# Swapping the operands of the products of keys' features with values: features stationary, values moving in 17 columns a head

## The chip, the cores and the metric

The kernel runs on one core of one Trainium2 chip. The metric is device time in microseconds (us) of one execution; the kernel before has a median of 490.55 us over three runs (489.4, 490.55 and 490.56).

## The reference, cut to what matters

The result mixes a linear attention `a` and a squared-ReLU feed-forward layer `b` with a gate of each row: `g * a + (1 - g) * b`. There are 2048 rows of 512 numbers, 32 heads of 16, and 1792 hidden units. The change touches the two sums over all rows, `kv` and `z`, in the attention:

```python
pk = jnp.einsum("bhsd,hdf->bhsf", k, w_phi)
phi_k = jnp.concatenate([_softmax(pk, axis=-1), _softmax(-pk, axis=-1)], axis=-1)   # 32 features a head
...
kv = jnp.einsum("bhsf,bhsd->bhfd", phi_k, v)     # per head 32 x 16
z  = jnp.einsum("bhsf->bhf", phi_k)              # per head 32
num = jnp.einsum("bhqf,bhfd->bhqd", phi_q, kv)
den = jnp.einsum("bhqf,bhf->bhq", phi_q, z)[..., None] + 1e-6
o = num / den
...
h = jnp.einsum("bsd,df->bsf", x, w1) + b1        # feed-forward, 512 to 1792
h = jnp.where(h > 0, h, 0) ** 2
b = jnp.einsum("bsf,fd->bsd", h, w2) + b2        # and back to 512
```

## The kernel before

All work is recorded first and ordered afterwards. A `Plan` object takes every operation of TensorE (PE), VectorE (DVE), ScalarE (ACT), GpSimd (POOL) and of the DMA queues of SyncE (SP) and ACT, finds what depends on what, and sets the order with a list scheduler that holds a table of lengths; PE's products go in groups, and at each step the scheduler takes the earliest startable of the next five groups. Some operations may go to either DVE or POOL (`nc.either`), and some DMAs to either queue (`nc.queues`); the scheduler picks. So a length that changes in one place can move operations elsewhere. All recorded operations carry line 359 in the profile, and one tells them apart by tiles.

The large products (the feed-forward and the projections) are made of three fp32r products of high and low parts (`h` and `l` in the tile names), and by a Strassen scheme (the `p1` to `p7` of the code). They write the banks uA, uE, uB (two of them), vA, vB, vE and kv, each 128 x 512.

The first half computes hidden units and, merged into it, keys and values for pairs of row blocks. For each of eight pairs of 128-row blocks the features of the keys stand in a tile `e` or `ez` (128 rows x 32 heads x 32 features) and the values in `vext` (128 rows x 32 heads x 17, the 17th column being one, so that the same product also gives `z`). `kv_burst` then makes 64 small fp32 products of them (two row blocks x 32 heads) into bank kv, four heads at a time in the four 32-column strips of the array, and adds the bank to the running sums in `kvs`. In the kernel before, the stationary operand is 32 columns of `vext`, starting at the head's first and reaching past its 17th, and the features are the 32 moving columns; in the bank a head has values along partitions and features along columns, so 17 of its 32 partitions mean something.

After the last burst, `kv_done` (line 724 and following) writes `z`, which stands on four partitions of `kvs`, to a row in DRAM (`zrow`) with two small DMAs, reads it back broadcast to 128 partitions into the two `vext` tiles (they are free by then) with two DMAs, turns `kvs` by two transposes on PE into a bank, and copies the sums from there into `kvb`, in four copies, block by block. The second half computes the queries' features chunk by chunk: `do_q` (product and exponentials), `transposed` (POOL multiplies by the broadcast z into `ez`, DVE sums and scales, a transpose to `tb`, then 12 DMAs and 4 ACT copies to `phiT`), `do_n` (products of `kvb` with `phiT`) and `attend`, all merged into the down projection of the feed-forward.

Of the kernel before, what the change touches and what calls it, by code (L numbers as in the profile page):

```python
# [10 lines left out]
AF = mybir.ActivationFunctionType  # L11
ALU = mybir.AluOpType
# [5 lines left out]
P = 128  # L18
S, D, H, DH, F = 2048, 512, 32, 16, 1792
# [5 lines left out]
NG = 8  # L25
VW = DH + 1
# [345 lines left out]
def tile_gated_mix(ctx: ExitStack, tc: tile.TileContext, xT, xn, wqT, wkT, wphi, wv, wo, w1, b1, w2, b2, gw, out):  # L372
    nc = Plan(tc.nc)
# [14 lines left out]
    def turn(*tags):  # L388
        i = turns[tags] = turns.get(tags, -1) + 1
        return banks[tags[i % len(tags)]]  # L390

    bank = lambda: turn("vA", "vB", "vE", "kv")
# [23 lines left out]
    const = lambda name, *shape: sbuf.tile([P, *shape], F32, tag=name, name=name)  # L416
    ident = const("ident", P)
# [4 lines left out]
    inv, eps, rest = (const(n, NB * NC) for n in ("inv", "eps", "rest"))  # L422
    kvb = const("kvb", NG, 2 * DH)
    tc.nc.gpsimd.memset(kvb, 0.0)
    kvs = const("kvs", 2 * P)
    tc.nc.gpsimd.memset(kvs, 0.0)
    zrow = dram.tile([2 * D], F32, name="zrow")
    xkept = dram.tile([6, 2, P, SB], F32, name="xkept")
# [270 lines left out]
    def kv_burst(v):  # L699
        n = 8 * v[0] + 2 * v[1]  # L700
        ps = banks["kv"]
        nc.product()
        for m in range(2):
            phi, ve = st["phi", n + m], vext[m]
            for i in range(NG):
                for j in range(4):
                    h = 8 * (i % 4) + 4 * (i // 4) + j
                    nc.tensor.matmul(ps[32 * j:32 * j + 32, 32 * i:32 * i + 32], ve[:, h * VW:h * VW + 32],
                                     phi[:, 32 * h:32 * h + 32], start=(m == 0 and i == 0), stop=(m == 1),
                                     skip_group_check=True)  # L710
        nc.vector.tensor_tensor(kvs, kvs, ps[:, :2 * P], ALU.add)

    def kv_done():
        zr = zrow.rearrange("(i q j f) -> q j i f", i=4, q=2, f=32)
        for q in range(2):
            nc.scalar.dma_start(zr[q], kvs[DH::32, q * P:(q + 1) * P].rearrange("p (i f) -> p i f", f=32))
        for half in range(2):
            nc.scalar.dma_start(vext[half][:, :D], zrow[half * D:(half + 1) * D].partition_broadcast(P))
        kvt = bank()
        nc.product()  # L720
        for i in range(2):
            nc.tensor.transpose(kvt[:, i * P:(i + 1) * P], kvs[:, i * P:(i + 1) * P], ident)
        kt = kvt[:, :2 * P].rearrange("p (g v) -> p g v", v=32)
        for j in range(4):
            s = slice(32 * j, 32 * j + 32)
            nc.vector.tensor_copy(kvb[s, :, DH * (j % 2):DH * (j % 2 + 1)], kt[s, :, :DH])

# [245 lines left out]
    def run(seq):  # L975
        for u, p in seq:
            if p == "burst":
                kv_burst(u)
            else:
                (v_step if len(u) == 3 else u_step)(u, p)  # L980
# [30 lines left out]
    fold("q", wqT, [t[:, k * D:(k + 1) * D] for k in range(NK)], load(ring(), wphi))  # L1011
    run(seq[-4:])
    kv_burst((1, NC - 1, "kv"))


# [6 lines left out]
    at = [0, 1, 5, 8, 11, 13, 16, 19, 22, 24, 27, 30, 33, 35, 38, 41]  # L1022
    wq_ready()
    when(1, kv_done)
    when(5, wo_ready)
    for i in range(NB):
        when(at[4 * i], gates, ORDER_B[i])
    for p in range(8):
# [3 lines left out]
        s = max(at[2 * p + 1], 2)  # L1032
# [3 lines left out]
    for t in range(NT):  # L1036
        for f in steps.get(t, ()):
            f()
        i, f = divmod(t, NF)
# [80 lines left out]
```

## Time and profile before

| | |
|---|---|
| runs | 489.4, 490.55, 490.56 us; median 490.55 |
| profiled execution | 490.21 us, of which the span of the profile is 488.4 us |
| PE busy | 482.6 us, 99% of the span, 3538 matmul records |
| DVE, ACT, POOL busy | 385.0, 251.2 and 160.1 us |
| granted TensorE clock | 1.000 of full speed over the span |
| DMA | 108.66 MB, mean 222 GB/s |

The time of the profiled execution is 1.8 us longer than its span, for what lies outside the first and last instruction. An fp32 product is two LDWEIGHTS and two MATMUL records; an fp32r product is one of each. Starts of instructions are in us from the span's start. A record's length is from its start to its modelled end, and successive matmuls overlap, so what a product costs is read from the distance between starts.

### The profile page before, as it was taken

Reading aid. Unit: us, or ns where it says so; the run is one execution under the profiler, and the core shown is the slowest. Engines: PE = TensorE matmul, PEld = TensorE weight load, DVE = VectorE, ACT = ScalarE, POOL = GpSimd, SP = SyncE. Lnnn points to the kernel's source line nnn. Section 1 sums busy time; section 2 is a strip of 40 time slices with the busy share of each in tenths; the row PEclk is TensorE's granted clock in tenths of the full one; section 3 lists DMA queues with packets and bytes.
Section 4 is the critical chain, followed back from the end, with each engine's and each line's share of the span. In section 5 each row is a group of like instructions: output and inputs, shape, how many; then the busy total and the mean of one; then the engine's idle time right before and its main releaser. Section 6 shows DMA issues by size and latency. Waiting matters only on the chain.

```text
span 488.4 us, 9588 instructions
## 1 busy us (share of the span) xinstructions
PE 482.6 (99%) x3538; PEld 389.2 (80%) x3538; DVE 385.0 (79%) x572; ACT 251.2 (51%) x447; POOL 160.1 (33%) x129
## 2 busy tenths in 40 slices
PE   9999999999999999999899999999999999999997
PEld 4878888888888888888788788787878788788786
DVE  3997999999987686969796799987795768996023
ACT  5897976579856664787510704133435213361210
POOL 1343165439520341246240434431621504261000
PEclk9999999999999999999999999999999999999999
DMA  7999999753787989898878576554317362354602
GB/s 275 382 401 364 374 329 344 268 175 131 243 267 274 313 258 326 275 321 305 279 214 226 138 266 185 194 172 119 119 41 192 136 180 91 89 159 137 229 25 86
DMA packets 65735, 108.66 MB, mean 222 GB/s; under 512 B 8216, under 2 KB 17688, under 8 KB 65688
## 3 DMA queue, kind: packets, MB, share of 16 engines
q1 hardware_dynamic: 60240, 102.66, 62.5%
q10 hardware_dynamic: 5416, 5.38, 4.2%
q8 instruction: 28, 0.46, 0.4%
q14 instruction: 19, 0.16, 0.1%
q0 software_dynamic: 32, 0.01, 0.0%
HBM read 60.30 MB, written 41.42 MB: 208 GB/s over the span
## 4 chain that ended last, share of the span: by engine, by line
PE 93%; DVE 3%; DMA 1%; ACT 1%; issue 1%; SPq 1%
PE uB L359 26%; PE uA L359 14%; PE uE L359 14%; PE vA L359 11%; PE vB L359 10%; PE kv L359 9%; PE vE L359 9%; DMA KT30h<-in_w 1%; SPq L359 1%; DVE oh L359 0%; DVE O1l L359 0%; DVE tb L359 0%; DVE KT31h L359 0%; DVE O0l L359 0%; DVE KB221l L359 0%
## 5 line engine op out<-in xcount | busy, mean ns | idle before, releaser
L359 POOL TENSOR_TENSOR ez<-e,vext 128x512 f32<-128x512 f32 x32 | 41.8, 1327 | 97.3 <-ACT e L359 85.2
L359 ACT ACTIVATE e<-e 128x512 f32<-128x512 f32 x54 | 32.0, 624 | 40.2 <-DVE e L359 40.1
L359 ACT ACTIVATE phiT<-tb 32x512 f32<-32x512 f32 x32 | 20.2, 630 | 52.2 <-DMA phiT<-tb 49.7
L359 DVE TENSOR_REDUCE sm<-e 128x64 f32<-128x1024 f32 x27 | 32.7, 1209 | 17.5 <-ACT e L359 17.3
L359 ACT ACTIVATE row<-row 128x512 f32<-128x512 f32 x56 | 34.0, 625 | 0.4
L359 POOL TENSOR_TENSOR row<-row,b2b 128x512 fp32r<-128x512 f32 (+1 forms) x12 | 17.0, 1419 | 38.3 <-ACT b2b L359 34.5
L359 DVE TENSOR_REDUCE ends<-vA 128x32 f32<-128x512 f32 x26 | 16.6, 681 | 9.7 <-PE vA L359 9.6
L359 POOL TENSOR_TENSOR row<-row,wo 128x512 fp32r<-128x512 f32 x10 | 14.0, 1401 | 27.7 <-ACT wo L359 27.7
L359 ACT ACTIVATE O0h<-ring 128x512 fp32r<-128x512 f32 x17 | 10.7, 627 | 21.9 <-DMA row<-in_wo 13.7
L359 DVE TENSOR_TENSOR e<-e,w 128x1024 f32<-128x1024 f32 x16 | 21.6, 1351 | 0.3
L359 DVE TENSOR_REDUCE dz<-ez 128x64 f32<-128x1024 f32 x16 | 19.3, 1206 | 3.0 <-POOL ez L359 3.0
L359 DVE STREAM_TRANSPOSE tb<-e 128x1024 f32<-128x1024 f32 x16 | 19.7, 1231 | 1.1 <-DMA O1l<-hkept 1.0
L359 DVE RECIPROCAL r<-sm 128x64 f32<-128x64 f32 x32 | 17.4, 544 | 0.4
L359 ACT ACTIVATE O1h<-ring 128x512 fp32r<-128x512 f32 x17 | 10.7, 628 | 12.7 <-PE uB L359 8.5
L359 ACT ACTIVATE wo<-row 128x512 fp32r<-128x512 f32 x17 | 10.6, 625 | 9.2 <-DMA hkept<-wo 9.1
L359 DVE TENSOR_TENSOR e<-e,r 128x1024 f32<-128x1024 f32 x11 | 14.0, 1273 | 0.1
L359 POOL TENSOR_TENSOR O1l<-ring,O1h 128x512 fp32r<-128x512 f32 x9 | 12.4, 1378 | 4.2 <-ACT O1h L359 4.2
L359 DVE TENSOR_TENSOR O0l<-ring,O0h 128x512 fp32r<-128x512 f32 x14 | 9.8, 704 | 4.5 <-ACT O0h L359 4.3
L359 ACT ACTIVATE oh<-vB 128x512 fp32r<-128x512 f32 x8 | 4.7, 593 | 15.7 <-PE vE L359 15.7
L359 DVE TENSOR_TENSOR row<-row,b2b 128x512 fp32r<-128x512 f32 (+1 forms) x12 | 8.1, 691 | 5.8 <-ACT b2b L359 5.8
L359 POOL TENSOR_TENSOR KB210h<-KB210h,KB211h 128x256 f32<-128x256 f32 x1 | 6.9, 6883 | 17.6 <-DVE KB211h L359 17.6
L359 DVE TENSOR_TENSOR O1l<-ring,O1h 128x512 fp32r<-128x512 f32 x8 | 6.3, 786 | 8.0 <-ACT O1h L359 8.0
(1157 smaller groups left out, 1701.3 us busy)
## 6 DMA issues: line engine op xcount, KB each, us to landing
hkept<-row SPq DMA_DIRECT2D x56, 256.0 KB, 4.9
ring<-hkept SPq DMA_DIRECT2D x24, 256.0 KB, 4.3
hkept<-b2b SPq DMA_DIRECT2D x16, 256.0 KB, 4.0
hkept<-wo SPq DMA_DIRECT2D x16, 256.0 KB, 3.6
xn<-in_xn SPq DMA_DIRECT2D x16, 256.0 KB, 3.8
O0h<-hkept SPq DMA_DIRECT2D x16, 256.0 KB, 3.2
O0l<-hkept SPq DMA_DIRECT2D x16, 256.0 KB, 3.5
O1h<-hkept SPq DMA_DIRECT2D x16, 256.0 KB, 4.4
```

What stands on the lines that cost most here:

```text
L359: call(*map(real, op.args), **{k: real(a) for k, a in op.kw.items()})
```

## The change

`kv_burst` swaps the operands: 32 features of a head are stationary and the head's 17 columns of `vext` move. The sums of a head now stand with features along partitions and 17 values along columns, eight heads beside each other on each strip of 32 partitions, and `kvs` has 136 columns and not 256. `kv_done` no longer turns `kvs`: `kvb` is filled by four copies straight from `kvs`. `z` now stands down the partitions, in column 16 of each group of 17, so it is turned by one transpose of 128 x 8 on PE, copied by ACT into a new tile `zt` (8 x 128), and written to `zrow` with one DMA. The two broadcast reads into `vext` stay.

```diff
-    kvs = const("kvs", 2 * P)
+    kvs = const("kvs", NG * VW)
+    zt = const("zt", P)
...
             phi, ve = st["phi", n + m], vext[m]
-            for i in range(NG):
-                for j in range(4):
-                    h = 8 * (i % 4) + 4 * (i // 4) + j
-                    nc.tensor.matmul(ps[32 * j:32 * j + 32, 32 * i:32 * i + 32], ve[:, h * VW:h * VW + 32],
-                                     phi[:, 32 * h:32 * h + 32], start=(m == 0 and i == 0), stop=(m == 1),
+            for b in range(NG):
+                for a in range(4):
+                    h = 8 * a + b
+                    nc.tensor.matmul(ps[32 * a:32 * a + 32, b * VW:(b + 1) * VW], phi[:, 32 * h:32 * h + 32],
+                                     ve[:, h * VW:(h + 1) * VW], start=(m == 0 and b == 0), stop=(m == 1),
                                      skip_group_check=True)
-        nc.vector.tensor_tensor(kvs, kvs, ps[:, :2 * P], ALU.add)
+        nc.vector.tensor_tensor(kvs, kvs, ps[:, :NG * VW], ALU.add)
 
     def kv_done():
-        zr = zrow.rearrange("(i q j f) -> q j i f", i=4, q=2, f=32)
-        for q in range(2):
-            nc.scalar.dma_start(zr[q], kvs[DH::32, q * P:(q + 1) * P].rearrange("p (i f) -> p i f", f=32))
+        kv = kvs.rearrange("p (b v) -> p b v", v=VW)
+        ps = bank()
+        nc.product()
+        nc.tensor.transpose(ps[:NG, :P], kv[:, :, DH], ident)
+        nc.scalar.activation(zt[:NG, :], ps[:NG, :P], AF.Copy)
+        nc.scalar.dma_start(zrow.rearrange("(a b f) -> b a f", a=4, f=32), zt[:NG, :].rearrange("b (a f) -> b a f", f=32))
         for half in range(2):
             nc.scalar.dma_start(vext[half][:, :D], zrow[half * D:(half + 1) * D].partition_broadcast(P))
-        kvt = bank()
-        nc.product()
-        for i in range(2):
-            nc.tensor.transpose(kvt[:, i * P:(i + 1) * P], kvs[:, i * P:(i + 1) * P], ident)
-        kt = kvt[:, :2 * P].rearrange("p (g v) -> p g v", v=32)
-        for j in range(4):
-            s = slice(32 * j, 32 * j + 32)
-            nc.vector.tensor_copy(kvb[s, :, DH * (j % 2):DH * (j % 2 + 1)], kt[s, :, :DH])
+        for a in range(4):
+            s = slice(32 * a, 32 * a + 32)
+            nc.vector.tensor_copy(kvb[s, :, DH * (a % 2):DH * (a % 2 + 1)], kv[s, :, :DH])
```

The scheduler's length of a small product is the same for 17 and 32 moving columns, but the shorter addition to `kvs` and the new steps of `kv_done` move other work. On PE three places differ: the shapes, the third burst (12 products later than before), and the stretch after the last burst. There, on PE, the two transposes (`vB<-ident,kvs`) stood behind the query product of the first chunk (into vA). Before:

```order
L359 MATMUL vA<-XS31l_3138,XA121h_1461 128x512 [waits DVE_49]
L359 MATMUL vA<-XS31h_3129,XA121l_1594 128x512
L359 MATMUL vB<-ident,kvs 128x128 x2
L359 MATMUL vE<-XS20h_3102,XA110h_1416 128x512
L359 MATMUL vE<-XS20l_3117,XA110h_1416 128x512
```

Now the one transpose stands ahead of both query products, directly behind the twelve products of the down projection that follow the burst, and six more of these, with the next hidden tile (O1h, O1l), come ahead of the queries:

```order
L359 MATMUL uB_73<-KB110h_2674,O0l_2663 128x512
L359 MATMUL vB<-ident,kvs 8x128 [waits DVE_49]
L359 MATMUL uA<-KB111h_2702,O1h_2707 128x512 [waits DMAHW7_49]
L359 MATMUL uA<-KB111l_2739,O1h_2707 128x512 [waits Pool_49]
L359 MATMUL uA<-KB111h_2702,O1l_2732 128x512 [waits DMAHW0_49]
L359 MATMUL uE<-KB111h_2702,O1h_2707 128x512
```

On ACT, which also issues these DMAs, the two writes of z stood among the splits of weights (`KB221h`, `KT40h`, `KT41h`). Before:

```order
L359 DMA zrow<-kvs 4x4x32 [waits DMAHW0_49,DVE_49]
L359 ACTIVATE KB221h_3141<-KT40l_2920 128x512 [waits DMAHW6_49]
L359 ACTIVATE KT40h_3147<-KT41l_2983 128x512 [waits DMAHW7_49]
L359 ACTIVATE row_3072<-row_3072 128x512 [waits Activation_49]
L359 DMA zrow<-kvs 4x4x32 [waits DMAHW2_49]
L359 ACTIVATE KT41h_3178<-ring_3120 128x512 [waits DMAHW7_49]
L359 DMA vext_98<-zrow 128x512 [waits DMAHW2_49,DMAHW6_49,DMAHW0_49,PE_49]
L359 DMA vext_99<-zrow 128x512 [waits PE_49]
```

Now the copy `zt`, which waits for PE, and the one write stand behind them:

```order
L359 ACTIVATE KB221h_3135<-KT40l_2921 128x512 [waits DMAHW6_49]
L359 ACTIVATE KT40h_3141<-KT41l_2975 128x512 [waits DMAHW7_49]
L359 ACTIVATE row_3073<-row_3073 128x512 [waits Activation_49]
L359 ACTIVATE zt<-vB 8x128 [waits PE_49]
L359 DMA zrow<-zt 8x4x32 [waits DMAHW1_49,Activation_49]
L359 ACTIVATE KT41h_3180<-ring_3120 128x512 [waits DMAHW7_49]
L359 DMA vext_99<-zrow 128x512 [waits DMAHW5_49,DMAHW1_49]
L359 DMA vext_100<-zrow 128x512
```

The broadcast reads keep their place in ACT's queue, but the value they wait for now comes through PE and ACT. On DVE the four copies to `kvb` move up to directly behind the last addition to `kvs`, between the splits XS20l to XS30l. From the second burst to about 250 us, DVE and POOL share the either-or work a little differently: POOL has 3 rows more, DVE 2 fewer.

## The prediction

> **What bounds the kernel.** I read the page first (shares, then the chain of waits), next what PE waits for, and last the bursts in the timeline and by stretches.
>
> ```profile
> PE 482.6 (99%) x3538; PEld 389.2 (80%) x3538; DVE 385.0 (79%) x572; ACT 251.2 (51%) x447; POOL 160.1 (33%) x129
> PE 93%; DVE 3%; DMA 1%; ACT 1%; issue 1%; SPq 1%
> ```
> ```profile
> PE kv L359 <- issue: 1.3, 1, 1.3
> PE uB L359 <- PEq L1109: 0.8, 1, 0.8
> ...
> PE uB L359 <- DVE vE L359: 0.2, 1, 0.2
> ```
>
> PE is the bound: it waits in all for little over 2 us, of which 1.3 us stand inside a burst and are put down to no releaser. So the change is worth what it takes from PE's own sequence, plus any wait it adds or takes away. What a burst costs there, in the second burst:
>
> ```profile
> 94.54 0.39 PE L359 MATMUL vA<-KB211l,XA121h 128*128 128x512 f32 x1
> 94.77 0.39 PE L359 MATMUL vA<-KB211h,XA121l 128*128 128x512 f32 x1
> 95.08 0.73 PE L359 MATMUL kv<-ez,vext 128*32 128x32 f32 x62
> ...
> 96.31 0.50 PE L359 MATMUL uB<-XS20h,O2h 128*128 128x512 f32 x1
> 96.65 0.40 PE L359 MATMUL uB<-XS20l,O2h 128*128 128x512 f32 x1
> ```
> ```profile
> 95.08:95.36 0.28, 0.27 (x32) 0.27 (x33) 0.00 (x0) 0.00 (x0) 1.00 1.10 425
> ...
> 95.76:95.96 0.20, 0.20 (x48) 0.20 (x37) 0.00 (x0) 0.00 (x0) 1.00 0.43 164
> ```
> ```profile
> L359 PE MATMUL kv<-e,vext x704: 189/196/217, 78.6 to 235.1; 128*32 128x32 f32 x176
> L359 PE MATMUL kv<-ez,vext x320: 190/196/217, 95.1 to 234.5; 128*32 128x32 f32 x160
> L359 PE MATMUL vB<-phiT,kvb x128: 376/376/400, 276.5 to 462.7; 64*32 64x256 f32 x128
> ```
>
> Products of 512 columns start 0.23 us apart (94.54, 94.77). The burst starts at 95.08 and the next product at 96.31, so eight bursts take 8 x 1.23 = 9.8 us, 2% of the time. The second fence counts kv's records per stretch (behind the two times: PE's busy time, then its records, which include those still running at the stretch's start). A head of 32 records starts within 0.27 us, 8.4 ns apart. After that, 48 records are seen in 0.20 us plus the 0.196 us that a record lasts: 8.25 ns apart, or 16.5 ns a product, since 704 + 320 = 1024 records are two for each of 512 products.
>
> **Does the rate follow the moving columns?** The fold of the queries' weights, where 32 x 32 blocks stand still and 128 columns move, separates columns from supply:
>
> ```profile
> 227.64 0.29 PE L359 MATMUL vA<-tb,ring 32*32 32x128 f32 x1
> ...
> 227.74 0.29 PE L359 MATMUL kv<-tb,ring 32*32 32x128 f32 x1
> ...
> 228.10 0.29 PE L359 MATMUL vE<-tb,ring 32*32 32x128 f32 x1
> 228.11 0.29 PE L359 MATMUL kv<-tb,ring 32*32 32x128 f32 x1
> ...
> 228.20 0.29 PE L359 MATMUL vA<-tb,ring 32*32 32x128 f32 x1
> ```
>
> At its head 16 records go to 16 blocks in 0.10 us, 6.7 ns apart. Later they come to blocks that stand empty and yet start 16.7 ns apart (228.10 to 228.20 in six steps). Nothing in the array holds them; they arrive at that pace. The burst's 16.5 ns a product is the same pace with a quarter of the columns. So I take both for the rate at which PE is supplied with fp32 products (their weights, 32 columns in both, included), which 17 columns leave as it is.
>
> **The sum, part by part.**
>
> *Bursts.* Bound for the gain: a record of 256 columns lasts 376 ns and one of 32 lasts 196, so a column is (376-196)/224 = 0.80 ns and 15 fewer are 12 ns a record; if the columns set the pace with four strips in turn, 12/4 = 3 ns x 1024 records = 3.1 us go. Lower bound: nothing. A loss isn't excluded, since operands at odd offsets now move. The nearest rows for it are the first burst and the second:
>
> ```profile
> 78.50:80.00 1.50, 1.41 (x128) 1.00 1.07 393
> 95.00:96.50 1.50, 1.30 (x128) 1.00 0.56 214
> ```
>
> By PE's busy time (the first number behind the length) bursts of the same form differ by 0.11 us, and 0.11 x 8 = 0.9 us. I take the supply reading: only the head can tighten, from 8.4 to 6.7 ns, 32 x 1.7 = 0.05 us a burst, 0.4 us in all.
>
> *Transposes.* Two full ones leave and a 128 x 8 one, in a 32-column strip, comes.
>
> ```profile
> 240.58 0.39 PE L359 MATMUL vA<-XS31h,XA121l 128*128 128x512 f32 x1
> 240.81 0.38 PE L359 MATMUL vB<-ident,kvs 128*128 128x128 f32 x2
> 240.95 0.48 PE L359 MATMUL vE<-XS20h,XA110h 128*128 128x512 f32 x1
> 241.26 0.39 PE L359 MATMUL vE<-XS20l,XA110h 128*128 128x512 f32 x1
> ```
>
> From 240.58 to 241.26 is 0.68 us where two steps of 0.23 would do: the two cost 0.22 us. A strip product costs its surroundings more: the burst is entered in 0.31 us (94.77 to 95.08) and left with a step of 0.34 (96.31 to 96.65). With 0.14 (240.81 to 240.95) to 0.31 between, the single one takes 0.79 to 0.96 against 0.46, so 0.33 to 0.50. Lower end: half of today's, 0.11. I take 0.33, nearest to the burst: +0.1 us net, ends -0.1 and +0.3.
>
> *Off PE.* Each addition to kvs falls from 128 x 256 to 128 x 136:
>
> ```profile
> L359 DVE TENSOR_TENSOR kvs<-kvs,kv x8: 409/414/422, 80.3 to 235.4; 128x256 f32<-128x256 f32 x8
> L359 DVE COPY kvb<-vB x4: 269/287/297, 242.2 to 244.2; 32x128 f32<-32x128 f32 x4
> ```
>
> At most 0.41 us leaves DVE per burst, and PE didn't wait for kvs; it is costed at nothing. The four copies (0.3 us each) now stand ahead of XS30l; three splits of 0.7, the addition and four copies are 3.6 us from 235.4, so XS30l is there at 239.0, while its product is the eighth of vA, behind the transpose and six products: 238.1 + 0.4 + 13 x 0.23 = 241.5. The six products moved ahead need O1l:
>
> ```profile
> 231.76 1.45 SPq L359 DMA_DIRECT2D O1l<-hkept  x1
> O1l<-hkept SPq DMA_DIRECT2D x1, 256.0 KB, 5.6
> 237.86 0.39 PE L359 MATMUL uB<-KB110h,O0l 128*128 128x512 f32 x1
> ```
>
> It lands at 231.76 + 5.6 = 237.4. The transpose starts one step behind 237.86, and O1l is first read three products later, past 238.7: 1.3 us of cover, else its lateness is paid in full. The remaining reshuffle of DVE and POOL I cost at nothing, with up to 0.5 us for a new wait, a few times the 0.2 us that PE now waits for DVE.
>
> *z.* This path gets longer:
>
> ```profile
> 237.05 0.52 ACTq L359 DMA_DIRECT2D zrow<-kvs  x1
> 238.03 0.61 ACT L359 ACTIVATE row<-row 128x512 f32<-128x512 f32 x1
> 239.74 0.91 ACTq L359 DMA_DIRECT2D vext<-zrow  x2
> 245.51 2.54 POOL L359 TENSOR_TENSOR ez<-e,vext 128x512 f32<-128x512 f32 x2 [3.92 <-DMA vext<-zrow]
> 269.50 2.57 ACT L359 ACTIVATE phiT<-tb 32x512 f32<-32x512 f32 x4 [5.81 <-DMA phiT<-tb]
> 276.51 0.40 PE L359 MATMUL vB<-phiT,kvb 64*32 64x256 f32 x1
> ```
>
> From the last write's issue to the reads is 2.7 us, and 5.8 more to POOL. The transpose ends near 238.4, the copy zt follows ACT's row (238.64) and ends near 239.0, so POOL starts near 239.0 + 2.7 + 5.8 = 247.5 instead of 245.5. Behind zt in ACT's queue stand the write, KT41h (whose load the change doesn't move), the reads, and the exponentials of the first chunk, whose product vA is itself six products later now. What z feeds ends with phiT at 272.1, and PE first reads it at 276.5: 2 us late into 4.4 us of cover, free.
>
> 490.21 - 0.4 + 0.1 = **489.9 us**, in the profiled execution's own time, which lies 0.34 below the median shown. Its own range is 489.2 to 490.6, the spread of the runs around it.
>
> **A rule against the change.** The trace gives 16.5 ns a product for 32 moving columns and 16.7 for 128. The Trainium skill (TensorEngine Tiling, Instruction Overhead) says that a matmul has an overhead of some 60 cycles, so that one column takes as long as 60. By it 17 columns are worth nothing and the sum would be 490.3; by the columns' row it would be 487.2. The trace agrees with the rule that columns don't count here, though its records follow each other at 6.7 ns at the fastest.
>
> **Rivals.**
> *Columns set the pace* (0.10): in the burst alone, the head's 8.4 ns and the later 8.25 ns look alike, and the head is not short of supply. It would be 490.21 - 3.1 + 0.1 = 487.2. Against it stands the fold's spacing on empty blocks.
> *The stall in the last burst goes* (0.12). It isn't the array's:
>
> ```profile
> 232.44 0.55 PE L359 MATMUL kv<-ez,vext 128*32 128x32 f32 x39
> 234.28 0.40 PE L359 MATMUL kv<-ez,vext 128*32 128x32 f32 x25 [1.29 <-issue]
> q8 instruction: 28, 0.46, 0.4%
> ```
>
> 28 packets of 16 KB, 0.46 MB, are 65 bytes for each of PE's 7076 records, so q8 looks like PE's code, and burst and fold use it up fast. Other traffic could let it come in time: 490.21 - 1.3 - 0.3 = 488.6. Against: both kernels have as many fp32 records in fold and burst.
> *Slower: z too late* (0.07). If the path z to phiT grows by over 4.4 us rather than 2, the first product with kvb waits at 276.5. At 6 us more (a second trip of 3.9 us through crowded queues) that is +1.6 on the forecast, or 491.5.
> *Slower: a stall of 1.3 us in another burst* (0.06), the third if any, as it moves by 12 products: 490.21 + 1.3 - 0.3 = 491.2. Against: no fold stands near it.
>
> The forecast has 0.65. The rivals of both signs set the range 488.2 to 491.3, which leaves out the columns' case and half of the late z. Under 0.3% (1.5 us) a change of this kernel can't be told from none, the runs themselves being 1.16 us apart. Faster by that: 0.10 for the columns, most of the stall's 0.12 and a little for the spread, 0.22; slower: the two slow cases in part, 0.09; same: 0.69.
>
> **What the profile after would show.** If I am right, a burst still takes 1.15 to 1.2 us from its first record to the next product and late records stay 16 to 17 ns a product apart; the transpose costs 0.3 to 0.5 us; POOL's first ez starts near 247.5 and PE doesn't wait for phiT or O1l; the 1.3 us stall stands in the last burst. A burst under 1.0 us makes the supply reading wrong; a named wait of PE near 238 or 276 makes the covers wrong.

## The result and the profile after

The changed kernel is slower: 492.9 us median (492.21 to 493.71, six runs) against 489.85 (489.4 to 490.56, six runs of the kernel before beside them), a ratio of 1.0061, 95% interval 1.0046 to 1.0076. I had forecast 489.9 with a range up to 491.3, so both the sign and the size were missed. The profiled execution took 493.71 us, its span is 491.9 us (488.4 before). Of all the runs below one was disturbed (689.66 us at a granted clock of 0.656, of the old products in the new order) and counts in no median or ratio.

On the page, the first row to look at is again the shares, and then the chain of work that ended last:

```profile
PE 484.4 (98%) x3537; PEld 388.5 (79%) x3537; DVE 385.1 (78%) x569; ACT 250.5 (51%) x448; POOL 156.5 (32%) x132
PE 90%; DMA 4%; DVE 3%; issue 1%; ACT 0%; SPq 0%; DVEq 0%
```

The chain now runs through DMA for 4% of the span where it had 1%. What PE waits for has become a list (us in total, times, longest):

```profile
PE kv L359 <- DVE phiT L359: 1.3, 1, 1.3
PE uB L359 <- PEq L1108: 0.8, 1, 0.8
PE uB L359 <- DVE vE L359: 0.7, 1, 0.7
PE uB L359 <- DMA O2h<-wkept: 0.5, 1, 0.5
PE vB L359 <- DVE e L359: 0.5, 1, 0.5
PE uB L359 <- ACT XS10h L359: 0.3, 1, 0.3
```

The 0.8 us on PEq, at the start, were there before; beyond them it was 1.3 us put down to no releaser and 0.2 us each for DVE and a load. The 1.3 us on DVE's `phiT` is a wait of the last burst: the transposing copy `phiT<-kv` reads the fold of the queries' weights out of bank kv, which that burst writes anew. The wait for `e` stands ahead of it, inside the fold.

The bursts take a little less, as was forecast, but by half of the forecast gain. The second one, from the timeline:

```profile
95.72 0.39 PE L359 MATMUL vA<-KB211h,XA121l 128*128 128x512 f32 x1
96.04 0.71 PE L359 MATMUL kv<-vext,ez 128*32 128x17 f32 x62
...
96.61 0.70 PE L359 MATMUL kv<-vext,e 128*32 128x17 f32 x62
97.25 0.50 PE L359 MATMUL uB<-XS20h,O2h 128*128 128x512 f32 x1
```

From the product ahead of the burst (95.72) to the one behind it (97.25) there are now 1.52 us; before, from 94.77 to 96.31, 1.54. The starts behind the rounding give 1.520 and 1.544, so 0.024 us a burst and 0.2 us in eight. It doesn't come from the head: record 33 starts 0.274 us behind the first in both. Of the 0.024 us, 0.012 stand between record 33 and record 49 (0.146 us after 0.158) and 0.012 between the last record and the next product (0.114 after 0.126).

The transposition, ahead of the next hidden tile's products:

```profile
241.15 0.40 PE L359 MATMUL uB<-KB110h,O0l 128*128 128x512 f32 x1
241.39 0.27 PE L359 MATMUL vB<-ident,kvs 128*8 128x128 f32 x1
241.41 0.48 PE L359 MATMUL uA<-KB111h,O1h 128*128 128x512 f32 x1
241.73 0.39 PE L359 MATMUL uA<-KB111l,O1h 128*128 128x512 f32 x1
```

From 241.15 to 241.73 is 0.58 us where two steps of 0.23 would do. The one transposition costs 0.12 us, the two cost 0.22: 0.10 us less.

The path of z, on POOL, ACT and PE:

```profile
250.53 2.55 POOL L359 TENSOR_TENSOR ez<-e,vext 128x512 f32<-128x512 f32 x2 [7.32 <-DMA vext<-zrow]
```
```profile
270.94 2.57 ACT L359 ACTIVATE phiT<-tb 32x512 f32<-32x512 f32 x4 [3.52 <-DMA phiT<-tb]
```
```profile
279.93 0.40 PE L359 MATMUL vB<-phiT,kvb 64*32 64x256 f32 x1
```

What z feeds ends at 273.5 and PE reads it at 279.9, without a wait: 6.4 us of cover, of 4.4 before.

So by the profile the named parts of the change are together worth -0.3 us, and the loss is elsewhere. The starts of the bursts divide the span. From the start of burst 1 to that of burst 7 the changed kernel takes 136.16 us (before 135.38); from burst 7 to the first product with `kvb` 64.15 us (before 62.57); from there to the end of PE's last product 208.67 us (before 208.67). The first burst starts 1.06 us later (79.62 after 78.56), though the order is the same up to there. That start wanders from profile to profile: 78.56 to 79.15 us in the four profiles of this study with the old products, 79.15 to 80.05 in the ten with the new ones. So a part of it may belong to the change; the first experiment, which has it too (79.21), tells whether it costs time.

The worst stretch is from burst 7 to burst 8. By stretches (length, then busy time and records of PE, PEld, DVE, ACT and POOL; the last three columns are the granted clock, the DMA share and GB/s), the changed kernel:

```profile
215.78:237.30 21.52, 19.44 (x324) 14.90 (x323) 17.09 (x26) 16.35 (x32) 12.90 (x10) 1.00 0.89 298
```

and the kernel before:

```profile
213.94:232.44 18.50, 18.50 (x324) 14.95 (x323) 16.22 (x25) 15.36 (x30) 12.39 (x11) 1.00 0.94 328
```

The same products take 3.0 us more. PE, busy all the time before, now stands still for 2.1 us of it: 1.3 for `phiT`, 0.5 for `e` and 0.3 for `XS10h`. The other 0.9 us are starts that come later with no gap behind the modelled end of the record ahead.

### The profile page after: what moved, and what is told of

Its sections match the earlier page's. It is cut to its first block, busy times and chain, and to the rows that moved or that the text cites. A ratio compares the mean times of both kernels' runs of the same rounds, so it can differ in the third digit from the quotient of the medians.

```text
span 491.9 us, 9592 instructions
## 1 busy us (share of the span) xinstructions
PE 484.4 (98%) x3537; PEld 388.5 (79%) x3537; DVE 385.1 (78%) x569; ACT 250.5 (51%) x448; POOL 156.5 (32%) x132
## 4 chain that ended last, share of the span: by engine, by line
PE 90%; DMA 4%; DVE 3%; issue 1%; ACT 0%; SPq 0%; DVEq 0%
PE uB L359 25%; PE uA L359 14%; PE uE L359 14%; PE vA L359 10%; PE vB L359 9%; PE vE L359 9%; PE kv L359 9%; DMA KB210l<-in_w 1%; DMA O2h<-wkept 1%; DMA KT20l<-in_w 1%; DMA KT40h<-in_wphi 1%; DVE tb L359 0%; DVE O3l L359 0%; SPq L359 0%; DVE O1l L359 0%
## 5 line engine op out<-in xcount | busy, mean ns | idle before, releaser
L359 DVE TENSOR_REDUCE ends<-vA 128x32 f32<-128x512 f32 x26 | 16.7, 680 | 7.0 <-PE vA L359 6.8
L359 DVE TENSOR_TENSOR e<-e,w 128x1024 f32<-128x1024 f32 x16 | 20.5, 1282 | 0.3
L359 POOL TENSOR_TENSOR O1l<-ring,O1h 128x512 fp32r<-128x512 f32 x11 | 14.9, 1358 | 16.2 <-ACT O1h L359 16.2
L359 ACT ACTIVATE b2b<-row 128x512 fp32r<-128x512 f32 x16 | 10.0, 624 | 6.3 <-DMA hkept<-b2b 5.7
L359 DVE SCALAR_TENSOR_TENSOR xn<-xn,gwb 128x512 f32<-128x512 f32 x16 | 12.9, 807 | 0.0
```

Source lines behind the costliest of these rows:

```text
L359: call(*map(real, op.args), **{k: real(a) for k, a in op.kw.items()})
```

## The experiments

The change has two sides. One is the products and what they feed. The other is that the scheduler, which lays out all engines' work by estimated lengths, has a shorter addition to `kvs` to reckon with: 136 elements and not 256, 0.13 us less by its formula for VectorE (0.001045 us an element). Everything behind the first burst is laid out anew. Three theories after the result: A, the new order is the whole loss; B, the swapped products or the new end of `kv` cost it; C, the tiles behind `kvs`, which lie 32 bytes further on in memory (`kvs` is 480 bytes a partition shorter, `zt` adds 512), slow the opening. For theory A the work in question is on ScalarE, VectorE and GpSimd between burst 7 and the fold. Each ratio below is to the kernel before, run again in the same session (medians of 489.36 to 489.96 us).

### The changed products in the old order

The instructions are those of the change; only the length that the scheduler takes for the addition is the old one. Up to the last burst the order is then that of the kernel before.

```diff
         nc.vector.tensor_tensor(kvs, kvs, ps[:, :NG * VW], ALU.add)
+        nc.ops[-1].size = 2 * P
```

> The changed kernel, with the scheduler told that the addition to kvs is 256 columns long, as before; so everything up to the last burst stands in the old order, and only the swap itself and the new end (one transpose, z by way of ACT) are left of the change. Theory A (the loss is the new order of DVE and POOL work between the second and the last burst): 489.2 to 490.2 us, level with the kernel before or a little faster, no wait of PE for DVE phiT or DMA O2h, a burst's step 1.52 us. Theory B (the swapped products or the new end cost the time): stays within 0.5 us of the changed kernel, 492.4 to 493.4. Theory C (the 32 bytes by which all later tiles are moved in memory slow the opening by 1 us): 490.5 to 491.2, with the first burst at 79.6 us rather than 78.6.

Measured: 489.45 us median (488.93 to 490.25, 11 runs), ratio 0.9997, interval 0.9986 to 1.0007. The loss is gone, with the swapped products, the new end and the moved tiles all in place; theories B and C fall as its cause. The same stretch from burst 7 to burst 8:

```profile
214.31:232.76 18.45, 18.45 (x323) 14.94 (x322) 16.22 (x25) 15.29 (x29) 12.37 (x10) 1.00 0.96 338
```

PE is busy through all of it, and the last burst takes 1.545 us from product to product.

### The old products in the new order

The reverse: the kernel before, whose addition is announced to the scheduler with the new length.

```diff
         nc.vector.tensor_tensor(kvs, kvs, ps[:, :2 * P], ALU.add)
+        nc.ops[-1].size = NG * VW
```

> The kernel before, its instructions unchanged, with the scheduler told that the addition to kvs is 136 columns long; so between the second and the last burst the work stands in the changed kernel's order, and neither the products nor the end of kv are changed. Theory A: 491.5 to 492.8 us, with PE waiting for DVE ahead of the last burst and near the fold. Theory B: level with the kernel before, 489.4 to 490.4. Theory C: also level with the kernel before.

Measured: 492.49 us (492.10 to 493.14, four runs), ratio 1.0061, interval 1.0048 to 1.0075, which is the whole loss of the change with none of its products. In its profile PE waits 1.3 us for `phiT` in the last burst, as in the changed kernel. Theory A holds.

### Four moving columns

The kernel of the first experiment with 4 of a head's 17 columns moving; the rest of the values' sums is left out.

```diff
-                    nc.tensor.matmul(ps[32 * a:32 * a + 32, b * VW:(b + 1) * VW], phi[:, 32 * h:32 * h + 32],
-                                     ve[:, h * VW:(h + 1) * VW], start=(m == 0 and b == 0), stop=(m == 1),
+                    nc.tensor.matmul(ps[32 * a:32 * a + 32, b * VW + 13:(b + 1) * VW], phi[:, 32 * h:32 * h + 32],
+                                     ve[:, h * VW + 13:(h + 1) * VW], start=(m == 0 and b == 0), stop=(m == 1),
```

> As e1, but only 4 of a head's 17 columns move (the last 3 of the values and the ones), so 13 of 16 value columns of kv are left out. If fp32 products come at a fixed pace, a burst's step (from the last product ahead to the first behind) stays within 0.05 us of the 1.52 us at 17 columns, and late records stay two in 16 to 17 ns. If columns set the pace it falls in proportion, below 1.3 us.

Measured: 489.18 us (one run), and in its profile:

```profile
95.39 0.39 PE L359 MATMUL vA<-KB211h,XA121l 128*128 128x512 f32 x1
95.70 0.70 PE L359 MATMUL kv<-vext,ez 128*32 128x4 f32 x63
...
96.88 0.50 PE L359 MATMUL uB<-XS20h,O2h 128*128 128x512 f32 x1
```

Product to product 1.498 us, after 1.520 with 17 columns and 1.544 with 32. So 28 columns fewer are worth 0.046 us, 0.7 ns a product: the pace isn't that of the columns. Here too record 33 starts 0.274 us behind the first; the whole gain lies, in two equal parts, behind the head and behind the last record.

### The sums eight columns wider

The changed kernel, with `kvs` laid out eight columns wider, so that what stands behind it in memory starts elsewhere.

```diff
-    kvs = const("kvs", NG * VW)
+    kvs = const("kvs", NG * VW + 8)[:, :NG * VW]
```

> The changed kernel with kvs made 8 columns wider (unused), so that all tiles behind it lie a multiple of 64 bytes from where they lay before. The order is the changed kernel's. Theory A: as the changed kernel, 492.4 to 493.4 us. Theory C: about 1 us less, 491.5 to 492.2, the first burst starting at 78.6 us and not 79.6.

Measured: 491.8 us (491.11 to 492.29), ratio 1.0046, interval 1.0033 to 1.0058, which overlaps that of the change. The time lies in the range that theory C gave, but not for its reason: the first burst starts at 79.66 and not at 78.6. What its profile has less than the change's lies elsewhere (135.31 and not 136.16 us from burst 1 to burst 7, 20.45 and not 21.52 from 7 to 8), and it is a single profile of each. Whether the wider `kvs` takes anything off the time stays open; that theory C isn't the cause rests on the first two experiments.

### What costs time in the new order

ScalarE's queue between burst 7 and the fold, in the changed kernel:

```profile
217.60 0.63 ACT L359 ACTIVATE wo<-row 128x512 fp32r<-128x512 f32 x1 [2.67 <-DMA hkept<-wo]
218.14 0.61 ACT L359 ACTIVATE KB111h<-KT20l 128x512 fp32r<-128x512 f32 x1
219.23 1.14 ACT L359 ACTIVATE ez<-ez 128x512 f32<-128x512 f32 x2
```

and in the old order:

```profile
213.38 0.62 ACT L359 ACTIVATE KB111h<-KT20l 128x512 fp32r<-128x512 f32 x1
215.01 1.14 ACT L359 ACTIVATE ez<-ez 128x512 f32<-128x512 f32 x2
216.05 0.62 ACT L359 ACTIVATE wo<-row 128x512 fp32r<-128x512 f32 x1
```

A split makes the high or the low part of a tile. `wo<-row` is a split of a hidden tile into its slot, and the slot is free only once an earlier tile in it has been stored (`hkept<-wo`). Put first, it waits 2.67 us for that store, and everything behind it in the queue waits too: the exponentials `ez` come 4.2 us later, 2.75 of them against the start of burst 7. VectorE stands behind the exponentials. Its rows in the changed kernel:

```profile
220.41 1.22 DVE L359 TENSOR_REDUCE sm<-ez 128x64 f32<-128x1024 f32 x1 [3.00 <-ACT ez L359]
...
230.42 1.46 DVE L359 TENSOR_TENSOR O3l<-ring,O3h 128x256 fp32r<-128x256 f32 x1
231.80 0.68 DVE L359 TENSOR_TENSOR KT30l<-KT31l,KT30h 128x512 fp32r<-128x512 f32 x1
...
234.70 1.91 DVE L359 TENSOR_TENSOR e<-e,r 128x1024 f32<-128x1024 f32 x1
236.54 0.70 DVE L359 STREAM_TRANSPOSE phiT<-kv 128x512 f32<-128x512 f32 x1
```

and in the old order:

```profile
216.62 1.21 DVE L359 TENSOR_REDUCE sm<-ez 128x64 f32<-128x1024 f32 x1
...
226.72 1.07 DVE L359 TENSOR_TENSOR KB211l<-KT30l,KB211h 128x512 fp32r<-128x512 f32 x1
...
230.34 1.31 DVE L359 TENSOR_TENSOR e<-e,r 128x1024 f32<-128x1024 f32 x1
231.58 0.70 DVE L359 STREAM_TRANSPOSE phiT<-kv 128x512 f32<-128x512 f32 x1
```

There are two differences. Ahead, an idle 3.00 us in front of `sm`. Behind, two splits, `O3l` and `KT30l` (1.46 + 0.68 us), which GpSimd had, in place of one, `KB211l` (1.07), and a longer `e<-e,r` (1.91 and not 1.31). `O3l` is longer than its work: GpSimd starts `KB211l` 0.1 us ahead of it (230.32), and in the twelve profiles with fp32 products the same form took 0.41 to 0.42 us in the 12 cases without such work of GpSimd beside it and 1.45 to 1.48 in the 4 with it. Counted from burst 7, VectorE reaches `phiT` after 20.76 us in the changed kernel and 17.27 in the old order, and the last burst waits for that. The next runs take these two apart; theory A1 is the wait, A2 the splits.

### The waiting split moved back

```diff
 ScalarE's queue, in the changed kernel's order
-wo<-row
 KB111h<-KT20l
 row<-uE,b1c
 ez<-ez x2
+wo<-row
```

> The changed kernel with one instruction of ScalarE's queue moved: the split wo<-row, which stands between burst 7 and the fold and waited 2.67 us for the store hkept<-wo, now stands behind the exponentials ez that it held up. Theory A1 (that wait at the head of ScalarE's queue makes VectorE 2.2 us late for the fold, and this is most of the loss): ez starts near 216.4 instead of 219.2, VectorE no longer idles 3 us ahead of sm<-ez, and 1.3 to 2.2 us come back, so about 490.3 to 491.2 us, a ratio of 1.001 to 1.0035 to the kernel before instead of 1.0061. Theory A2 (the loss is the two splits O3l and KT30l that came to VectorE for KB211l): less than 0.5 us comes back, over 492.0 us and a ratio over 1.005.

What depends on the split moves with it. Measured: 491.53 us (490.28 to 492.57), ratio 1.0037, interval 1.0023 to 1.0051: 0.24% of the 0.61% come back, 1.2 us. That lies between the two expectations, just short of A1's 1.3 to 2.2 us, and the interval still touches that of the change (1.0046 to 1.0076). `ez` and `sm` are early again and VectorE reaches `phiT` 18.92 us after burst 7 and not 20.76. The wait of the last burst has hardly shrunk, since PE comes to it earlier too: it no longer waits for `e` and `XS10h`:

```profile
216.56 1.14 ACT L372 ACTIVATE ez<-ez 128x512 f32<-128x512 f32 x2
```
```profile
217.74 1.22 DVE L372 TENSOR_REDUCE sm<-ez 128x64 f32<-128x1024 f32 x1 [0.64 <-ACT ez L372]
```
```profile
PE kv L372 <- DVE phiT L372: 1.2, 1, 1.2
```

### The three splits back on their engines

```diff
 VectorE, in the changed kernel's order
-O3l<-ring,O3h
-KT30l<-KT31l,KT30h
+KB211l<-KT30l,KB211h
 GpSimd
-KB211l<-KT30l,KB211h
+O3l<-ring,O3h
+KT30l<-KT31l,KT30h
```

> The changed kernel with three splits put back on the engines they had before: O3l and KT30l to GpSimd, KB211l to VectorE; ScalarE's order stays as in the changed kernel. Theory A2 (these carry the loss: 1.46 + 0.68 us in place of 1.07, and e<-e,r at 1.91 instead of 1.31 us beside a busy GpSimd, 1.7 us on VectorE's way to phiT): 1.2 to 1.7 us come back, 490.8 to 491.3 us, ratio about 1.0025 to 1.0035. Theory A1 (the wait of wo): VectorE stays 2.2 us late, at most 1 us comes back, 491.5 us or more, ratio 1.004 or more.

Measured: 491.4 us (490.66 to 491.61), ratio 1.0031, interval 1.0019 to 1.0043: 0.30% come back, as theory A2 had it, although `wo` still waits (1.76 us here). PE's wait for `phiT` is halved:

```profile
PE kv L370 <- DVE phiT L370: 0.6, 1, 0.6
```

### Both

```diff
 both edits above, ScalarE and VectorE/GpSimd
```

> Both edits together: wo behind the exponentials, and the three splits back on their engines. If the two causes together are the loss, the time is that of the changed kernel in the old order, 489.2 to 489.9 us, ratio 0.9990 to 1.0010, and the step from burst 7 to burst 8 is near 18.5 us instead of 21.5. If some other part of the new order costs time too (the parts ahead of burst 7), it stays at 490.5 us or more.

Measured: 490.28 us (489.35 to 491.81, 12 runs), ratio 1.0014, interval 1.0004 to 1.0025. Of the 0.61%, 0.47% are back. PE waits no more for `phiT` by name, and burst 8 starts 18.61 us after burst 7, as expected. The time lies between the two expectations, and the interval touches that of the old order (0.9986 to 1.0007).

### And the gate's product

The third difference on VectorE: `xn<-xn,gwb`, which in the old order fills the gap ahead of `sm` and in the new one stands behind it.

```diff
 VectorE, with both put back
+xn<-xn,gwb
 sm<-ez
-xn<-xn,gwb
 r<-sm
```

> The kernel with wo and the three splits put back, and a third instruction moved: on VectorE the gate's product xn<-xn,gwb stands ahead of the sum sm<-ez again, in the gap in which VectorE waits for the exponentials. With both put back it stood behind sm and took 1.28 us there, and VectorE came to phiT 17.85 us after burst 7 began, against 17.27 in the old order. Theory: these three instructions' places and engines are the loss between burst 7 and the fold. Then the step from the start of burst 7 to the product behind burst 8 falls from 20.3 to about 19.9 us (20.0 in the old order) and the time to 489.6 to 490.0 us, ratio 0.9998 to 1.0010. Rival (what is left of the loss lies ahead of burst 7 only): no change, 490.2 us or more, ratio 1.0012 or more.

Measured: 490.49 us (489.56 to 491.17), ratio 1.0013, interval 1.0002 to 1.0023: nothing. What VectorE gains behind `sm` turns into another wait, a few rows on:

```profile
217.59 1.21 DVE L395 TENSOR_REDUCE sm<-ez 128x64 f32<-128x1024 f32 x1
...
221.16 0.81 DVE L395 TENSOR_SCALAR inv<-ge 128x4 f32<-128x4 f32 x1 [1.23 <-ACT ge L395]
```

`ge` stands behind seven others that follow the exponentials in ScalarE's queue, and comes no earlier. My theory of three causes falls at the third; the remaining 0.13% are placed only in part. The table below has 0.5 us more between bursts 1 and 7 than in the old order, which would be 0.1%, but these are single profiles. 0.2 us of it is steady: from burst 2 to burst 4 the six profiles of the change and of its repairs have 42.51 to 42.55 us, the two with the same products in the old order 42.29.

### The wait alone, in the old order

The kernel of the first experiment, with one instruction moved.

```diff
 ScalarE's queue, in the old order
+wo<-row
 KB111h<-KT20l
 row<-uE,b1c
 ez<-ez x2
-wo<-row
```

> The reverse trial: the changed products in the old order, with the one split wo<-row moved ahead of KB111h, row<-uE and the exponentials on ScalarE, as the new order has it. In the old order's run the store issued at 211.15 landed at 214.87, so wo would wait some 1.4 us, and ez would start 1.1 to 1.5 us later. Theory A1: VectorE comes 0.6 to 1.5 us late to the fold, 490.1 to 491.0 us, ratio 1.001 to 1.003. Theory A2: no change, 489.2 to 489.8 us, ratio within 0.9990 to 1.0008.

Measured: 490.14 us (489.44 to 491.17, 11 runs), ratio 1.0010, interval 1.0000 to 1.0020, at the edge of what can be told. The mechanism shows in the trace. The store was issued at 210.47 and landed at 214.42, 3.95 us later; in the changed kernel's profile it took 5.87 us (211.65 to 217.52), so there `wo` waited longer:

```profile
214.50 0.63 ACT L369 ACTIVATE wo<-row 128x512 fp32r<-128x512 f32 x1 [1.15 <-DMA hkept<-wo]
215.04 0.61 ACT L369 ACTIVATE KB111h<-KT20l 128x512 fp32r<-128x512 f32 x1
216.13 1.14 ACT L369 ACTIVATE ez<-ez 128x512 f32<-128x512 f32 x2
```

VectorE reaches `phiT` 17.98 us after burst 7, 0.71 later than in the old order, and PE waits 0.2 us for it in the last burst. The expectation for A1, 490.1 to 491.0 us, holds at its lower end; the intervals of this kernel and the old order (0.9986 to 1.0007) overlap.

Together, from the starts of the bursts in each profile, in us ("last step": from the product ahead of burst 8 to the one behind it; a wait right ahead of burst 8 is in "7 to 8" and in "last step"):

| kernel | ratio | burst 1 to 7 | 7 to 8 | last step | 7 to first product with kvb |
|---|---|---|---|---|---|
| the change | 1.0061 | 136.16 | 21.52 | 2.93 | 64.15 |
| wo moved back | 1.0037 | 135.42 | 19.68 | 2.77 | 62.30 |
| three splits back | 1.0031 | 135.95 | 19.34 | 2.22 | 62.20 |
| both | 1.0014 | 135.77 | 18.61 | 1.71 | 61.48 |
| both and xn | 1.0013 | 135.57 | 18.60 | 1.95 | 61.47 |
| old order, wo ahead | 1.0010 | 135.05 | 18.73 | 1.83 | 61.58 |
| old order | 0.9997 | 135.10 | 18.45 | 1.55 | 60.90 |
| kernel before | 1 | 135.38 | 18.50 | 3.11 | 62.57 |

Each of the two edits takes 1.9 us off the last column, both together 2.7 of the 3.25 between the change and the old order. Both shorten VectorE's way to the same `phiT`, so they overlap in part.

### The kernel before once more

> The kernel before, once more, for its profile. If the 1.3 us stall in the last burst (put down to no releaser) belongs to the kernel's code, it stands there again: the last burst's step to the next product is 3.1 us. If it is a chance of the run, the step is near 1.6 us and the span is shorter by up to 1.3 us, 487.1 us. The time is 489.0 to 490.7 us either way.

Measured: 490.37 us (one run), span 488.6 us. The stall in the last burst stands there again, at the same product:

```profile
233.07 0.55 PE L359 MATMUL kv<-ez,vext 128*32 128x32 f32 x39
234.43 0.40 PE L359 MATMUL kv<-ez,vext 128*32 128x32 f32 x25 [0.81 <-issue]
```

The last step is 2.62 us: neither the 3.1 nor the 1.6 expected, with a stall of 0.8 us and not 1.3. So the stall is no chance of one run, though its length varies, and the changed products in the old order don't have it (1.55). Their last step is 1.1 to 1.6 us shorter by it, yet the timed runs of the two differ by 0.14 us, with an interval of -0.7 to +0.3. Whether the stall is shorter in executions without a profile, and what causes it, stays open.

### What sets the pace of a burst

The changed products in the old order, each operand read as the upper half of its fp32 number. A pass is one weight load with one matmul record; a product on halves is one pass, an fp32 product two. The keys' sums lose precision.

```diff
-                    nc.tensor.matmul(ps[32 * a:32 * a + 32, b * VW:(b + 1) * VW], phi[:, 32 * h:32 * h + 32],
-                                     ve[:, h * VW:(h + 1) * VW], start=(m == 0 and b == 0), stop=(m == 1),
+                    nc.tensor.matmul(ps[32 * a:32 * a + 32, b * VW:(b + 1) * VW], phi.bitcast(mybir.dt.bfloat16)[:, 64 * h + 1:64 * h + 64:2],
+                                     ve.bitcast(mybir.dt.bfloat16)[:, 2 * h * VW + 1:2 * (h + 1) * VW:2], start=(m == 0 and b == 0), stop=(m == 1),
```

> The changed products in the old order, their operands read as the upper halves of the fp32 numbers (bfloat16): every product of a burst then is one pass with a load of weights of its own, in place of the fp32 product's two records. This lowers the precision of the keys' sums. Theory S1 (the pace of 16.7 ns is two passes of 8.3 ns each): 64 products a burst lose 8.3 ns each, the step from the product ahead of a burst to the one behind it falls from 1.520 to about 1.0 us, eight bursts gain 4 us, 485.3 us. Theory S2 (the pace is that of the instructions or of the weight loads, however wide the numbers): the step stays within 0.1 us of 1.52, or grows, since loads of weights are instructions of their own here; 489.0 us or more.

Measured: 485.75 us (485.48 to 485.85), ratio 0.9919, interval 0.9905 to 0.9932.

```profile
94.83 0.39 PE L359 MATMUL vA<-KB211h,XA121l 128*128 128x512 f32 x1
95.15 0.38 PE L359 MATMUL kv<-vext,ez 128*32 128x17 bf16 x32
95.37 0.43 PE L359 MATMUL kv<-vext,e 128*32 128x17 bf16 x32
95.73 0.50 PE L359 MATMUL uB<-XS20h,O2h 128*128 128x512 f32 x1
```

The step is 0.900 us, 0.62 us less than 1.520, and late products start 8.2 ns apart. The profile has 3025 weight loads and as many matmul records, 512 fewer of each than the 3537 in fp32: the 16.7 ns of an fp32 product are two passes of 8.3 ns. Theory S1 holds, at 0.62 and not 0.53 us, since the head tightens too (32 records in 0.218 us after 0.274). Which half of a pass sets the 8.3 ns, the weight load or the matmul, isn't told by this, as both are halved, and so are the bytes of the operands. Eight such steps would be 5.0 us, and the median is 4.2 below 489.96: in the profile the gain of the last two bursts is lost again, as from burst 7 to the first product with `kvb` it takes 60.88 us and in fp32 60.90, with a wait of 0.56 us for `XS30l`.

Then the same halves in the kernel before (`vext` still, 32 features moving):

```diff
-                    nc.tensor.matmul(ps[32 * j:32 * j + 32, 32 * i:32 * i + 32], ve[:, h * VW:h * VW + 32],
-                                     phi[:, 32 * h:32 * h + 32], start=(m == 0 and i == 0), stop=(m == 1),
+                    nc.tensor.matmul(ps[32 * j:32 * j + 32, 32 * i:32 * i + 32], ve.bitcast(mybir.dt.bfloat16)[:, 2 * h * VW + 1:2 * h * VW + 64:2],
+                                     phi.bitcast(mybir.dt.bfloat16)[:, 64 * h + 1:64 * h + 64:2], start=(m == 0 and i == 0), stop=(m == 1),
```

> The kernel before, its burst products likewise on the upper halves of the operands (bfloat16): values' 32 columns stand still and 32 columns of features move, at one pass a product. It lowers the precision of the keys' sums as the changed products on halves did, which took 0.900 us from the product ahead of a burst to the one behind it, late products 8.2 ns apart, 485.75 us. Theory S (the pace is one pass every 8.2 ns, and the form doesn't matter): the step is 0.90 to 0.94 us and the time 485.6 to 486.4 us, level with the changed products on halves. Theory K (at half the passes the moving columns count, 12 ns more over four strips, 3 ns a product): the step grows by up to 0.2 us to 1.1 us, 1.5 us in eight bursts, about 487.3 us.

Measured: 484.95 us (484.49 to 485.5), ratio 0.9905, interval 0.9888 to 0.9921.

```profile
94.68 0.39 PE L359 MATMUL vA<-KB211h,XA121l 128*128 128x512 f32 x1
95.00 0.38 PE L359 MATMUL kv<-ez,vext 128*32 128x32 bf16 x32
95.22 0.45 PE L359 MATMUL kv<-e,vext 128*32 128x32 bf16 x32
95.60 0.50 PE L359 MATMUL uB<-XS20h,O2h 128*128 128x512 f32 x1
```

The step is 0.912 us: 15 more columns cost 0.012 us at half the passes, after 0.024 at both. Theory S holds by the step; the time is 0.65 us below its range, and by the ratios (0.9905 and 0.9919, intervals that overlap) the change gains nothing there either. Both kernels on halves beat both kernels of this study by 0.8% and more, at bfloat16's precision in the keys' sums, which decides whether they may be used.

## Why the prediction was wrong

*The step that failed* is the sentence "The remaining reshuffle of DVE and POOL I cost at nothing, with up to 0.5 us for a new wait". The old products in the new order price it at 0.61% of 489.6 us, 3.0 us: six times its upper bound. What the runs show in its place is VectorE coming 3.5 us late to `phiT` (20.76 and not 17.27 us after burst 7), and PE late with it. The sentence also left out an engine: of the two parts that the runs show, one is the three splits that changed places between VectorE and GpSimd (0.30% come back with them), the other a single instruction on ScalarE that moved ahead of four others in its queue (0.24%). They overlap; together they are 0.47 of the 0.61%, and of the rest 0.2 us are placed (bursts 2 to 4), the remainder stays open.

I bounded the term by what PE waited for before (0.2 us), which tells how good the old order was and nothing of the new one. What could have been looked at is each instruction that moved ahead on a queue worked in order, when what it needs is there (here a store's landing), and who stands behind it; the landing itself, 5.87 us in one order and 3.72 in the other, would still have been a guess. The range's upper end, 491.3, was set by a late z and a stall; both rivals that could have given a slower time had the wrong mechanism. The sign named for wrong covers, a wait of PE by name near 238, did come (237.3), but on `phiT`, which no cover of the prediction was about.

*Bursts: right on the pace, wrong on where the gain is.* The pace doesn't follow the columns: 1.498, 1.520 and 1.544 us at 4, 17 and 32. I had 0.05 us a burst by a tighter head; it is 0.024, 0.2 us in all and not 0.4, and the head is as it was (0.274 us). The gain is twice 15 columns at the 0.80 ns of the columns' case, paid once behind the head and once at the end of a burst and not by each record. The columns' case (487.2) was rightly held against. The rule of the Trainium skill (TensorEngine Tiling, Instruction Overhead), by which columns under some 60 count for nothing, gave the right answer on columns, but for these 0.024 us a burst. What one sees here is a price for each pass: a product on halves costs half of an fp32 one at the same 17 columns.

*Transposes: the sign was wrong.* I took +0.1 us; it is -0.10. The single transposition costs 0.12 us, close to the lower end of 0.11 (half of the two), and not the burst's price: it is entered in 0.24 us and not 0.31, and the next product starts 0.02 us behind it.

*Kvs, kvb, O1l, z: right.* In none of the profiles does PE wait for `kvb`, `O1l` or the `phiT` of the second half. The cover of `XS30l`, 2.5 us by the prediction, holds in the changed kernel, but in four of the other kernels PE waits 0.15 to 0.56 us for it. In the old order, which has the new path of z, ACT issues the reads of z at 242.13 us, after 239.74 and 240.96 in the two profiles of the kernel before (1.2 to 2.4 us later, where 2 were forecast), and POOL starts `ez` at 246.11, after 245.51 and 246.06; what came late was covered.

*The stall.* It went, as the rival with 0.12 said; that the supply of code was its cause isn't shown. In the new order PE waits there for `phiT` instead, and in the old order its absence isn't seen in the timed runs.

## What to carry to other kernels

When a scheduler lays out the program by estimated lengths, the price of an edit has a second part: what the new estimate does to all work behind it. Do the edit in the old layout and the old code in the new layout; these two runs split it. Here an addition that the formula made 0.13 us shorter cost 3 us; the parts that were edited gained 0.3 us by the profile, which the timed runs are too coarse to show (ratio 0.9997, interval 0.9986 to 1.0007).

In a queue that is worked in order, an instruction that waits for a store's landing is best put behind those on the path to the bottleneck, even if it is due first: moved back, it gave 0.24% here; moved ahead in the old order, it cost 0.10%, at the edge of what can be told.

Small products in 32-column strips were paid by the pass here: half the passes gain 0.62 us in a burst of 64, 28 of 32 moving columns fewer only 0.05 us.

## What the runs showed of the hardware

- A burst of 64 fp32 products, 32 stationary columns each, runs at 8.3 ns a pass and two passes a product, for 4, 17 and 32 moving columns alike; in bfloat16 a product is one pass, and the burst takes 0.900 and 0.912 us against 1.520 and 1.544.
- VectorE and GpSimd stretch each other where both work on two operands from memory: on VectorE the same `e<-e,r` took 1.31 or 1.91 us and `O3l` of 128 x 256 took 1.46 us, longer than `KB211l` of 128 x 512 (1.07) in the other order. Over the twelve profiles with fp32 products `e<-e,r` took 1.15 to 1.23 us in the 94 cases with no such work of GpSimd beside it and 1.21 to 2.15 in the 38 with some; GpSimd's `XS10l` took 2.27 us beside `e<-e,r` in the changed kernel and 1.29 beside copies of one operand in the old order.
